# A new order for the first block of a fused FNet mixing and feed-forward kernel

## The chip, the cores and the metric

One core of a Trainium2 chip runs the whole kernel. Time is the device time of one execution in microseconds (us), the median over several executions. Beside it stands a profile of one more execution, taken by the hardware profiler: its span runs from the first to the last instruction.

The engines are TensorE (PE; PEld are its weight loads), VectorE (DVE), ScalarE (ACT), GpSimd (POOL) and SyncE (SP). Each has a queue of its own and works it off in order; semaphores tie them together.

## The reference

For x of 8 batches, 3008 rows and 256 columns, a Fourier transform over rows and columns, of which the real part is kept, and then a feed-forward layer with a squared ReLU:

```
X = np.fft.fft(x, axis=1)
X = np.fft.fft(X, axis=2)
x = X.real.reshape(8 * 3008, 256)
h = np.maximum(x @ w_in, 0.0)        # w_in 256 x 2048
out = h * h @ w_out                  # w_out 2048 x 256
```

## The kernel before

**What is computed in which form.** The transform over the 256 columns is never made by itself: its cosine and sine matrices (`c_all`, `s_n`) are multiplied with `w_in` once, which gives the weights `gh` (three groups of rows: cosine, sine, and a third that is the sine group times −2, called the turn). The transform over the 3008 rows uses symmetries. Rows n and S − n are added and subtracted (the tiles `u`, `v`, `cs`, `od`, `ev`), so that a quarter of the rows is left, and matmuls with tables of cosines and sines give `pz` in PSUM; copies of it are the tiles `zc` and `zs`, one column for each frequency. The first layer is then `gh[0]·zc + gh[1]·zs` for frequency k, and adding `gh[2]·zs` turns the same PSUM tile into the value for frequency S − k.

**Windows.** The frequencies of all batches stand in one row of columns, cut into windows of at most 512 columns (the first has 240). In a window the hidden 2048 rows come in eight steps of two blocks of 128. A step makes `ph` (L834, L835), a relu on ScalarE (L866), the turn matmuls (L857), a second relu, and a square on VectorE (L873). The second layer of a window (L685, tile `po`) is spread between the steps of the next one. Window 0 has its own form: four quads of four blocks each. `quad` (L912, L913) makes cosine and sine parts, `quad_relu` (L925) is one relu of a whole quad, `quad_turn` (L919) the turn, `quad_power` (L929) the square. There are two PSUM tiles for `ph`, so quad 2 waits until the second relu of quad 0 has read its tile.

**The order.** Nothing plans the work: the scheduling is manual and each engine's queue has the order in which the program issues the instructions. The first block is written out by hand:

1. GpSimd issues the load of the first batch's x in four quarters (`load_x`: two by one direct transfer, L127, two by gathers, L132), then `w_in` (L179) and later `w_out` (L318).
2. The tables of cosines and sines. For each angle n·k the whole turns are taken off: `args` (L231, ScalarE) scales and rounds, `turns` (L237) makes −S times the number of turns, `mods` (L243, VectorE) is n·k plus that, in three instructions for each of two halves. `sins` (L249, ScalarE) takes the sine. `weigh` (L270, ScalarE) scales one row of the sines. `coss` gets the cosines from the sines: a matmul with a mask that reverses the partitions (`perm`, L259, tile `pc`) and a copy (L260).
3. `idle` issues matmuls whose result nobody reads (L296, tile `pw`).
4. The fold of the first batch: `u_odd` (L388 to L390: quarter 0 minus 1, quarter 2 minus 3), `u_part` (L393, then L362, which gives `od`), a copy of one column of `od` on ScalarE (L396, the edge), `nyq` (two tiny matmuls and L444).
5. The matmuls `pz` of the first unit (L569). Each of the parts 0 (cosine) and 1 (sine) has two halves; between them ScalarE copies the first to `es` (L574), and behind them to `zc` or `zs` (L580 for window 0, L587 for window 1). `minus` (L598) gives the second half of the unit's columns.
6. The weights: `gh_step` (L515 matmuls `pg`; L505 scales on VectorE, L503 on ScalarE) for four groups of 512 columns, and `gh_turn` (L522).
7. `v_even` (L399) makes `v` and at its end issues the load of the next batch's x, which goes into the same tile. `d_even` (L419, L420) is the first to read that.

In window 1 the squares are kept back in a list: `settle` issues all that are in it. The steps of the next batch's fold lie between them, up to `nyq` (L444), which the matmuls `pz` of the second unit wait for.

Of the kernel before, what the change touches and what calls it, by code (L numbers as in the profile page):

```python
# [16 lines left out]
P = 128  # L17
# [12 lines left out]
def kernel(  # L30
# [130 lines left out]
    def iota(shape, pattern, base, mult, name):  # L161
        t = const.tile(shape, I32, name=name)
        nc.gpsimd.iota(t, pattern=pattern, base=base, channel_multiplier=mult)
        return t
# [9 lines left out]
        idx["r"] = iota([P, 1], [[1, 1]], P - 1, -1, "idx_r")  # L174

    xs = {0: load_x(0, idx_first)}
    w16 = [wp.tile([P, 2, F // 2], F16, name=f"w16_{i}", tag="w16") for i in range(2)]
    for i in range(2):
        nc.gpsimd.dma_start(out=w16[i], in_=moe_w_in[:, i * F // 2 : (i + 1) * F // 2].rearrange("(c p) f -> p c f", p=P))  # L179
# [2 lines left out]
    def small(shape, name):  # L182
        return const.tile(shape, F32, name=name)
# [22 lines left out]
    def table_steps(e):  # L206
# [28 lines left out]
        def turns(h, eng=nc.vector):  # L235
            t = st["t", h]
            eng.tensor_scalar(out=t[:, 0:nr, 0:n], in0=t[:, 0:nr, 0:n], scalar1=-R23, scalar2=-float(S), op0=ALU.add, op1=ALU.mult)  # L237

        def mods(h):
            m = st["m", h] = tmp.tile([P, 3, NE], F32, name="m", tag="tm")  # L240
            for j in range(nr):
                r = row(h, j)
                nc.vector.scalar_tensor_tensor(out=m[:, j, 0:n], in0=st["kf"], scalar=vec[:, r : r + 1], in1=st["t", h][:, j, 0:n], op0=ALU.mult, op1=ALU.add)  # L243
# [18 lines left out]
        def weigh():  # L262
            if e:
                for t in (cos_t, sin_t):
                    for r in range(2):
                        nc.vector.tensor_scalar(out=t[:, r, :], in0=t[:, r, :], scalar1=wge[:, r : r + 1], scalar2=None, op0=ALU.mult)
                return

            q = RQ.index(1)
            nc.scalar.activation(sin_t[:, q, :], sin_t[:, q, :], AF.Copy, bias=0.0, scale=wgt)  # L270

        return {"freq": freq, "args": args, "turns": turns, "mods": mods, "absm": absm, "sins": sins, "coss": coss, "weigh": weigh}

    to = table_steps(0)
    to["freq"]()
# [17 lines left out]
    def idle(n):  # L293

        for i in range(n):
            nc.tensor.matmul(pw[:, 0 : 3 * P], spn[:, 0, 0, :], spn.rearrange("p c r d -> p (c r d)")[:, 0 : 3 * P], start=True, stop=True)  # L296

    idle(34)
    to["args"](0)
    to["args"](1)  # L300
    wd = 2.0 * math.pi / D
    s_n = const.tile([P, 2, P + 1], F16, name="s_n")
    nc.scalar.activation(s_n, am, AF.Sin, bias=0.0, scale=-wd)
    c_all = const.tile([P, 2, P + 1], F16, name="c_all")
    nc.scalar.activation(c_all, at, AF.Sin, bias=halfpi[:, 0:1], scale=-wd)
    nc.scalar.activation(s_n[:, :, 0:1], c_all[:, :, P : P + 1], AF.Copy, bias=0.0, scale=0.5)

    to["turns"](0)
    to["mods"](0)
    to["turns"](1, nc.gpsimd)  # L310
    nc.gpsimd.tensor_scalar(out=wgt, in0=nraw[:, 1:2], scalar1=float(Q), scalar2=-0.5, op0=ALU.is_equal, op1=ALU.mult)
    nc.gpsimd.tensor_scalar(out=wgt, in0=wgt, scalar1=1.0, scalar2=None, op0=ALU.add)

    prow_i = iota([P, P], [[1, P]], 0, 1, "prow_i")
    perm = [const.tile([P, P], F16, name=f"perm{i}") for i in range(2)]
    for i in (1, 0):
        nc.gpsimd.tensor_scalar(out=perm[i], in0=prow_i, scalar1=float(P - 1 - i), scalar2=None, op0=ALU.is_equal)
    nc.gpsimd.dma_start(out=wout16, in_=moe_w_out.rearrange("(c p) o -> p c o", p=P))  # L318
    pick = const.tile([P, 1], F16, name="pick")
    nc.gpsimd.memset(pick, 0.0)  # L320
    nc.gpsimd.memset(pick[0:1, :], -2.0)
    evec_i = iota([P, 2], [[1, 2]], 0, 2, "evec_i")
    idx["c"] = iota([P, 1], [[1, 1]], P - 1, -1, "idx_c")
    nc.gpsimd.memset(idx["c"][0:2, :], P - 3)
# [10 lines left out]
    nc.gpsimd.tensor_tensor(wge, wge, wg2, op=ALU.add)  # L335
    nc.gpsimd.tensor_scalar(out=wg2, in0=evec, scalar1=0.0, scalar2=-0.5, op0=ALU.is_equal, op1=ALU.mult)
    nc.gpsimd.tensor_tensor(wge, wge, wg2, op=ALU.add)
    to["sins"](0)
    to["weigh"]()
    to["mods"](1)  # L340
    to["sins"](1)
    to["coss"](0)
    idle(4)
    to["coss"](1)
    to["coss"](2)
    idle(5)

    folded = {}

    fe = fo = None  # L350
# [13 lines left out]
    def fold_steps(i):  # L364
# [19 lines left out]
            fof = fo.rearrange("p q c d -> p (q c) d")  # L384


        def u_odd():
            nc.vector.tensor_tensor(u[:, 0], t[:, 0], t[:, 1], op=ALU.subtract)  # L388
            nc.vector.tensor_copy(t[0:1, 2, 0, :], t[0:1, 0, R - 1, :])
            nc.vector.tensor_tensor(u[:, 1], t[:, 2], t[:, 3], op=ALU.subtract)  # L390

        def u_part(sg):
            nc.vector.tensor_tensor(cs[:, sg], u[:, 0], rev_dim(u[:, 1], 1), op=ALU.subtract if sg else ALU.add)  # L393
            d_fold(od[:, sg], cs[:, sg], sg)
            if not sg:
                nc.scalar.activation(od[:, 0, :, 0:1], cs[:, 0, :, 0:1], AF.Copy, bias=0.0, scale=1.0)  # L396

        def v_even():
            nc.vector.tensor_tensor(v, tq[:, :, 0], tq[:, :, 1], op=ALU.add)  # L399
# [94 lines left out]
            nc.vector.tensor_copy(spn[:, :, :, 0:1], rev_dim(yt[:, :, 0, :, 128:129], 1))  # L494

        late = [lambda: fold8(0), lambda: fold8(1), lambda: fold16(0), lambda: fold16(1), nyq8]
        return {"u_odd": u_odd, "u_part": u_part, "v_even": v_even, "v_part": v_part, "d_even": d_even, "n_cos": n_cos, "odds": odds, "d_odd": d_odd, "load": load, "n_sin": n_sin, "nyq": nyq, "even": even, "away": away, "back": back, "late": late}

    gh = const.tile([P, 3, F], F16, name="gh")

# [19 lines left out]
    def gh_turn(cc):  # L520
        f0 = cc * 512
        nc.vector.tensor_scalar(out=gh[:, 2, f0 : f0 + 512], in0=gh[:, 1, f0 : f0 + 512], scalar1=turn2[:, 0:1], scalar2=None, op0=ALU.mult)  # L522
# [105 lines left out]
    def run(*jobs):  # L628
        for j in jobs:
            j()  # L630

    f0s = fold_steps(0)
    z0 = z_steps(need[0][0], late=True)
    run(f0s["u_odd"], lambda: f0s["u_part"](0))
    run(*z0(0, 0))
    gh_pg = gh_step(0)
    run(lambda: f0s["u_part"](1), f0s["nyq"])
    gh_scale(gh[:, 0:2, 0:512], gh_pg, False)
    run(*z0(0, 1))
    run(*z0(1, 0))  # L640
    run(*z0(1, 1))
    gh_step(1, False)
    turn2 = small([P, 1], "turn2")
    nc.vector.tensor_scalar(out=turn2, in0=dvec[:, 0:1], scalar1=0.0, scalar2=2.0, op0=ALU.is_equal, op1=ALU.mult)
    nc.vector.tensor_scalar(out=turn2, in0=turn2, scalar1=-2.0, scalar2=None, op0=ALU.add)
    gh_turn(0)
    gh_turn(1)

    def store(osb, p0, g0, m, minus, eng=nc.sync):

# [145 lines left out]
    for w in range(NW):  # L796
# [109 lines left out]

        def quad(p):
            ph = phs[p] = ps_h.tile([P, 2, 512], F32, name="ph", tag="psh")
            for c in range(4):
                f0 = (4 * p + c) * P  # L910
                o = ph[:, c // 2, (c % 2) * wn : (c % 2 + 1) * wn]
                nc.tensor.matmul(o, gh[:, 0, f0 : f0 + P], zcw[:, 0:wn], start=(c % 2 == 0), stop=False, skip_group_check=True)  # L912
                nc.tensor.matmul(o, gh[:, 1, f0 : f0 + P], zsw[:, 0:wn], start=False, stop=True, skip_group_check=True)  # L913

        def quad_turn(p):
            for c in range(4):
                f0 = (4 * p + c) * P
                o = phs[p][:, c // 2, (c % 2) * wn : (c % 2 + 1) * wn]
                nc.tensor.matmul(o, gh[:, 2, f0 : f0 + P], zsw[:, 0:wn], start=False, stop=True, skip_group_check=True)  # L919
# [9 lines left out]
            nc.vector.tensor_tensor(h, h, h, op=ALU.mult)  # L929

        if w == 0:
            rm = z0(0, 2) + z0(1, 2)
            run(lambda: quad(0), lambda: quad_relu(0, 0), lambda: quad(1), lambda: quad_relu(1, 0), f0s["v_even"])
            run(lambda: quad_turn(0), lambda: quad_relu(0, 1), lambda: gh_step(2, True), lambda: gh_turn(2))
            run(lambda: quad_power(0), lambda: quad_turn(1), lambda: quad_relu(1, 1), *rm[0::2])
            run(lambda: quad(2), lambda: quad_relu(2, 0), lambda: gh_step(3, False), lambda: gh_turn(3), lambda: quad_power(1))
            run(lambda: quad(3), lambda: quad_relu(3, 0), *rm[1::2])
            run(lambda: quad_turn(2), lambda: quad_relu(2, 1), lambda: quad_power(2), lambda: quad_turn(3), lambda: quad_relu(3, 1), lambda: quad_power(3))
        elif w == 1:
            zl = [j for zu, part, h in zj for j in zu(part, h)]  # L940
            for p in range(NST // 2):
                s0, s1 = 2 * p, 2 * p + 1
                f2q = spread(f2, p, NST // 2)
                n = len(f2q) // 4
                pq(s0)
                if p < 2:
                    settle()
                relu(s0, 0)
                pq(s1)
                relu(s1, 0)  # L950
                if s1 == NST - 1:
                    run(*post[s0 - 1])
                    settle()
                    power(s1, 0, 1)
                    run(*zl)
                run(*f2q[0:n])
                turn(s0)
                run(*f2q[n : 2 * n])
                turn(s1)
                relu(s0, 1)  # L960
                relu(s1, 1)
                run(*at[s0], *at[s1], *f2q[2 * n :])
                if p == 2:
                    settle()
                keep(s0, 0, 2)
                keep(s1, int(s1 == NST - 1), 2)
            gh_nyq()
# [68 lines left out]
```

## Time and profile before

| | us |
|---|---|
| three runs: median (lowest to highest) | 603.12 (602.83 to 603.47) |
| the profiled execution | 602.28 |
| its span, first to last instruction | 600.5 |
| TensorE busy in it | 585.7 (98%) |
| VectorE, ScalarE, GpSimd busy | 497.4, 458.5, 242.5 |
| first matmul of pz | at 15.48 |
| first relu of window 0, end of its last | 20.93, 31.14 |
| window 1's first matmul | at 30.34 |

The mean granted TensorE clock was 0.997 of full speed. A row of a timeline has the start and length in us, engine, line, operation, what is written from what, the tile's shape and the count; in brackets stands the idle time before it and what ended it. A row of the chain of waits has start, length, engine, tile and line. A row of the waits has who waited for whom, the sum in us, how often, and the longest.

### The profile page before, as it was taken

The numbers are of one execution on the slowest core, as the hardware profiler recorded it, in microseconds if no ns is written. First come the engines' busy times: TensorE is split into PE (matmuls) and PEld (weight loads), VectorE is DVE, ScalarE is ACT, GpSimd is POOL, SyncE is SP. The second block draws the span as 40 slices with busy tenths as digits, with TensorE's granted clock in tenths as the row PEclk, the third lists the DMA queues.
The fourth block names the chain that finished last, engine by engine and source line by source line (L and its number), as shares of the span: only waits on it lengthen the run. The fifth ranks groups of instructions, "written<-read, shape, count | busy, mean of one in ns | idle before, by whom it ended". The sixth has DMA issues, their size and how long they took to land.

```text
span 600.5 us, 11262 instructions
## 1 busy us (share of the span) xinstructions
PE 585.7 (98%) x4415; PEld 424.2 (71%) x4415; DVE 497.4 (83%) x594; ACT 458.5 (76%) x613; POOL 242.5 (40%) x285
## 2 busy tenths in 40 slices
PE   7899999999999999999999999999999999999997
PEld 3457776677776767777777777777777777777786
DVE  8787688997989878969899798988899888889871
ACT  6687777967887877778778778777877787787762
POOL 8311355078415515183153641445505724325210
PEclk8999999999999999999999999999999999999999
DMA  8946421127212461273123711146212321212212
GB/s 149 151 85 151 119 74 44 43 84 171 65 38 59 112 155 45 70 151 104 40 62 100 164 47 52 47 118 143 64 34 86 86 63 36 61 41 54 61 55 70
DMA packets 37624, 50.33 MB, mean 84 GB/s; under 512 B 4589, under 2 KB 30755, under 8 KB 37571
## 3 DMA queue, kind: packets, MB, share of 16 engines
q0 software_dynamic: 10400, 24.94, 20.5%
q1 hardware_dynamic: 26899, 24.44, 13.6%
q8 instruction: 34, 0.56, 0.4%
q10 hardware_dynamic: 272, 0.23, 0.1%
q14 instruction: 19, 0.16, 0.1%
HBM read 36.42 MB, written 27.86 MB: 107 GB/s over the span
## 4 chain that ended last, share of the span: by engine, by line
PE 80%; DVE 11%; ACT 4%; issue 2%; DMA 1%; POOL 1%; ACTq 0%; DVEq 0%; POOLq 0%
PE po L685 47%; PE ph L857 6%; PE ph L834 6%; PE ph L835 6%; PE ph L852 5%; PE ph L843 5%; PE pz L569 4%; DVE h L873 3%; DVE t L847 2%; DVE h L864 2%; ACT h L866 2%; DMA xo<-in_x_dram,idx_r 1%; ACT h L877 1%; DVE zc L598 1%; DVE zs L598 1%
## 5 line engine op out<-in xcount | busy, mean ns | idle before, releaser
L685 PE MATMUL po<-wout,h 128*128 128x256 f16 (+1 forms) x3024 | 363.5, 273 | 0.0
L685 PEld LDWEIGHTS <-h 128*128 128x128 f16 (+1 forms) x3024 | 296.7, 98 | 73.5
L866 ACT ACTIVATE h<-ph 128x1024 f16<-128x1024 f32 (+3 forms) x303 | 288.9, 991 | 60.9 <-PE ph L852 37.3
L873 DVE TENSOR_TENSOR h<-h 128x2048 f16<-128x2048 f16 (+7 forms) x201 | 194.4, 973 | 19.1 <-ACT h L866 15.8
L793 POOL TENSOR_SCALAR n<-zn,g2n 128x512 f32<-128x512 f16 (+3 forms) x162 | 160.4, 1004 | 73.4 <-DMA zn<-rd 53.7
L847 DVE SCALAR_TENSOR_TENSOR t<-ph,n 128x1024 f32<-128x1024 f32 (+3 forms) x81 | 96.4, 1190 | 34.7 <-PE ph L843 31.4
L864 DVE CUSTOM_DVE_ANT_0 h<-t,ph 128x1024 f16<-128x1024 f32 x71 | 86.5, 1218 | 22.8 <-ACT h L866 20.0
L700 ACT ACTIVATE osb<-po 128x512 f32<-128x512 f32 (+3 forms) x95 | 55.0, 582 | 51.7 <-PE po L685 43.9
L785 POOL DMA_DIRECT2D zn<-rd x22 | 12.8, 584 | 179.1 <-DMA rd<-zs 179.1
L834 PE MATMUL ph<-zc,gh 128*128 128x512 f16 (+3 forms) x222 | 81.9, 369 | 2.1 <-DVE zc L598 1.1
L877 ACT ACTIVATE h<-h 128x1024 f16<-128x1024 f16 (+3 forms) x81 | 83.8, 1034 | 0.3
L835 PE MATMUL ph<-zs,gh 128*128 128x512 f16 (+3 forms) x222 | 81.9, 369 | 0.0
L857 PE MATMUL ph<-zs,gh 128*128 128x512 f16 (+3 forms) x222 | 63.8, 369 | 0.0
L852 PE MATMUL ph<-zs,gh 128*128 128x512 f16 (+3 forms) x162 | 47.0, 372 | 1.5 <-issue 0.5
L843 PE MATMUL ph<-zc,gh 128*128 128x512 f16 (+3 forms) x162 | 47.1, 372 | 0.0
L834 PEld LDWEIGHTS <-gh 128*128 128x128 f16 x222 | 21.6, 97 | 25.1 <-DVE zc L598 1.4
L835 PEld LDWEIGHTS <-gh 128*128 128x128 f16 x222 | 21.7, 98 | 24.2 <-issue 1.5
L843 PEld LDWEIGHTS <-gh 128*128 128x128 f16 x162 | 15.8, 98 | 18.4 <-issue 0.7
L857 PEld LDWEIGHTS <-gh 128*128 128x128 f16 x222 | 20.6, 98 | 3.5
L453 POOL DMA_DIRECT2D scr<-ev x8 | 4.7, 590 | 40.8 <-DVE ev L449 34.9
L463 POOL DMA_INDIRECT rb<-scr,idx_r x16 | 18.3, 1141 | 4.9 <-issue 4.9
L574 ACT ACTIVATE es<-pz 128x376 f32<-128x376 f32 (+1 forms) x32 | 14.8, 485 | 7.0 <-PE pz L569 6.8
(141 smaller groups left out, 366.0 us busy)
## 6 DMA issues: line engine op xcount, KB each, us to landing
out_dram<-osb SPq DMA_DIRECT2D x77, 128.0 KB
xo<-in_x_dram POOLq DMA_DIRECT2D x7, 768.0 KB
scr<-ev POOLq DMA_DIRECT2D x8, 390.0 KB
zn<-rd POOLq DMA_DIRECT2D x19, 128.0 KB
rb<-scr POOLq DMA_DIRECT2D x16, 130.0 KB
out_dram<-osb SPq DMA_DIRECT2D x12, 94.0 KB
w<-in_moe_w_in_dram POOLq DMA_DIRECT2D x2, 512.0 KB
wout<-in_moe_w_out_dram POOLq DMA_DIRECT2D x1, 1024.0 KB
```

What stands on the lines that cost most here:

```text
L685: nc.tensor.matmul(po[0:m, j * D : (j + 1) * D], h2[:, fc, q : q + m], wout16[:, fc, :], start=(fc == 0 and not both), stop=(fc == NFC - 1 ...
L793: nc.gpsimd.tensor_scalar(out=n2[:, a, 0:wn1], in0=zns[wt][:, 0:wn1], scalar1=g2n[:, fc : fc + 1], scalar2=1.0, op0=ALU.mult, op1=ALU.mult)
L834: nc.tensor.matmul(ph[:, a, 0:wn], gh[:, 0, f0 : f0 + P], zcw[:, 0:wn], start=True, stop=False)
L835: nc.tensor.matmul(ph[:, a, 0:wn], gh[:, 1, f0 : f0 + P], zsw[:, 0:wn], start=False, stop=True)
L843: nc.tensor.matmul(ph[:, a, 0:wn], gh[:, 0, f0 : f0 + P], zcw[:, 0:wn], start=True, stop=True)
L847: nc.vector.scalar_tensor_tensor(out=t2[:, :, 0:wn], in0=phs[s][:, :, 0:wn], scalar=-2.0, in1=n2s[w, s][:, :, 0:wn], op0=ALU.mult, op1=ALU ...
L852: nc.tensor.matmul(phs[s][:, a, 0:wn], gh[:, 1, f0 : f0 + P], zsw[:, 0:wn], start=False, stop=True, skip_group_check=True)
L857: nc.tensor.matmul(phs[s][:, a, 0:wn], gh[:, 2, f0 : f0 + P], zsw[:, 0:wn], start=False, stop=True, skip_group_check=True)
L864: nc.vector._custom_dve(TENSOR_ADD_SAT, out=h, in0=t2s[s][:, :, 0:wn], in1=phs[s][:, :, 0:wn], s0=BIG, s1=0.0)
L866: nc.scalar.activation(h, phs[s][:, :, 0:wn], AF.Relu, bias=0.0, scale=-1.0)
L873: nc.vector.tensor_tensor(h, h, h, op=ALU.mult)
L877: nc.scalar.activation(h, h, AF.Square, bias=0.0, scale=1.0)
```

## The change

- **Angles.** For the second half of the angles the instructions of `mods` go. `kns` makes n·k on ScalarE (three copies with a scale), `sums` adds the turns on GpSimd in one instruction over the whole tile.
- **Other engines.** `weigh` goes from ScalarE to GpSimd; the two instructions for `wgt` and the two masks `perm` go from GpSimd to VectorE; `turn2` (two tiny instructions) from VectorE to GpSimd. The iota `prow_i` is issued ahead of the load of `w_in`; `w_out` is issued behind `weigh`.
- **Fold.** `u_odd` is cut into `u_half` (quarters 0 and 1, and the copy of one row) and `u_odd` (quarters 2 and 3). `coss` is issued behind `u_part(0)`; the edge copy becomes a step of its own, behind `coss`.
- **TensorE.** 44 idle matmuls instead of 34 ahead of the first `coss`.
- **Weights and unit.** `gh_turn(0)` and `gh_step(1)` are issued between the two halves of part 1 of `pz`; the copies of `zc` and `zs` for window 1 directly behind the half whose result they read, ahead of window 0; `v_even` behind `gh_turn(1)`, ahead of window 0.
- **Window 0.** A quad makes its four cosine matmuls first and then its four sine matmuls. `gh_step(2)` goes ahead of the first turn, `gh_step(3)` ahead of quad 2, and both are scaled on VectorE. The four squares come at the end.
- **Window 1.** Behind the third pair of steps one kept square is issued instead of all that are kept (two at that point).

```diff
     xs = {0: load_x(0, idx_first)}
+    prow_i = iota([P, P], [[1, P]], 0, 1, "prow_i")
...
+        def kns(h):
+            m = st["m", h] = tmp.tile([P, 3, NE], F32, name="m", tag="tm")
+            for j in range(nr):
+                r = row(h, j)
+                nc.scalar.activation(m[:, j, 0:n], st["kf"], AF.Copy, bias=0.0, scale=vec[:, r : r + 1])
+
+        def sums(h):
+            m = st["m", h][:, 0:nr, 0:n]
+            nc.gpsimd.tensor_tensor(m, m, st["t", h][:, 0:nr, 0:n], op=ALU.add)
...
             q = RQ.index(1)
-            nc.scalar.activation(sin_t[:, q, :], sin_t[:, q, :], AF.Copy, bias=0.0, scale=wgt)
+            nc.gpsimd.tensor_scalar(out=sin_t[:, q, :], in0=sin_t[:, q, :], scalar1=wgt[:, 0:1], scalar2=1.0, op0=ALU.mult, op1=ALU.mult)
...
-    idle(34)
+    idle(44)
     to["args"](0)
     to["args"](1)
+    to["kns"](1)
...
-    nc.scalar.activation(s_n[:, :, 0:1], c_all[:, :, P : P + 1], AF.Copy, bias=0.0, scale=0.5)
     to["turns"](0)
     to["mods"](0)
     to["turns"](1, nc.gpsimd)
-    nc.gpsimd.tensor_scalar(out=wgt, ...
-    prow_i = iota([P, P], [[1, P]], 0, 1, "prow_i")
+    to["sums"](1)
+    nc.vector.tensor_scalar(out=wgt, ...
     for i in (1, 0):
-        nc.gpsimd.tensor_scalar(out=perm[i], in0=prow_i, ...
+        nc.vector.tensor_scalar(out=perm[i], in0=prow_i, ...
+    to["sins"](0)
+    nc.scalar.activation(s_n[:, :, 0:1], c_all[:, :, P : P + 1], AF.Copy, bias=0.0, scale=0.5)
+    to["weigh"]()
     nc.gpsimd.dma_start(out=wout16, in_=moe_w_out.rearrange("(c p) o -> p c o", p=P))
...
+    nc.gpsimd.tensor_scalar(out=turn2, ...
...
-    to["sins"](0)
-    to["weigh"]()
-    to["mods"](1)
     to["sins"](1)
-    to["coss"](0)
-    idle(4)
-    to["coss"](1)
-    to["coss"](2)
-    idle(5)
...
-        def u_odd():
+        def u_half():
             nc.vector.tensor_tensor(u[:, 0], t[:, 0], t[:, 1], op=ALU.subtract)
             nc.vector.tensor_copy(t[0:1, 2, 0, :], t[0:1, 0, R - 1, :])
+
+        def u_odd():
             nc.vector.tensor_tensor(u[:, 1], t[:, 2], t[:, 3], op=ALU.subtract)
...
-    run(f0s["u_odd"], lambda: f0s["u_part"](0))
+    run(f0s["u_half"], f0s["u_odd"], lambda: f0s["u_part"](0))
+    to["coss"](0)
+    idle(4)
+    to["coss"](1)
+    to["coss"](2)
+    idle(5)
+    f0s["edge"]()
     run(*z0(0, 0))
     gh_pg = gh_step(0)
     run(lambda: f0s["u_part"](1), f0s["nyq"])
     gh_scale(gh[:, 0:2, 0:512], gh_pg, False)
     run(*z0(0, 1))
     run(*z0(1, 0))
+    gh_turn(0)
+    gh_step(1, False)
+    rm = z0(0, 2) + z0(1, 2)
+    rm[0]()
     run(*z0(1, 1))
-    gh_step(1, False)
-    turn2 = small([P, 1], "turn2")
...
-    gh_turn(0)
+    rm[2]()
     gh_turn(1)
+    f0s["v_even"]()
...
-            for c in range(4):
-                f0 = (4 * p + c) * P
-                o = ph[:, c // 2, (c % 2) * wn : (c % 2 + 1) * wn]
-                nc.tensor.matmul(o, gh[:, 0, f0 : f0 + P], zcw[:, 0:wn], start=(c % 2 == 0), stop=False, skip_group_check=True)
-                nc.tensor.matmul(o, gh[:, 1, f0 : f0 + P], zsw[:, 0:wn], start=False, stop=True, skip_group_check=True)
+            for k, zw in ((0, zcw), (1, zsw)):
+                for c in range(4):
+                    f0 = (4 * p + c) * P
+                    o = ph[:, c // 2, (c % 2) * wn : (c % 2 + 1) * wn]
+                    nc.tensor.matmul(o, gh[:, k, f0 : f0 + P], zw[:, 0:wn], start=(k == 0 and c % 2 == 0), stop=(k == 1), skip_group_check=True)
...
         if w == 0:
-            rm = z0(0, 2) + z0(1, 2)
-            run(lambda: quad(0), lambda: quad_relu(0, 0), lambda: quad(1), lambda: quad_relu(1, 0), f0s["v_even"])
-            run(lambda: quad_turn(0), lambda: quad_relu(0, 1), lambda: gh_step(2, True), lambda: gh_turn(2))
-            run(lambda: quad_power(0), lambda: quad_turn(1), lambda: quad_relu(1, 1), *rm[0::2])
-            run(lambda: quad(2), lambda: quad_relu(2, 0), lambda: gh_step(3, False), lambda: gh_turn(3), lambda: quad_power(1))
-            run(lambda: quad(3), lambda: quad_relu(3, 0), *rm[1::2])
-            run(lambda: quad_turn(2), lambda: quad_relu(2, 1), lambda: quad_power(2), lambda: quad_turn(3), lambda: quad_relu(3, 1), lambda: quad_power(3))
+            run(lambda: quad(0), lambda: quad_relu(0, 0), lambda: quad(1), lambda: quad_relu(1, 0))
+            run(lambda: gh_step(2, False), lambda: gh_turn(2))
+            run(lambda: quad_turn(0), lambda: quad_relu(0, 1), lambda: quad_turn(1), lambda: quad_relu(1, 1))
+            run(lambda: gh_step(3, False), lambda: gh_turn(3))
+            run(lambda: quad(2), lambda: quad_relu(2, 0), lambda: quad(3), lambda: quad_relu(3, 0), *rm[1::2])
+            run(lambda: quad_turn(2), lambda: quad_relu(2, 1), lambda: quad_turn(3), lambda: quad_relu(3, 1), *(lambda p=p: quad_power(p) for p in range(4)))
...
                 if p == 2:
-                    settle()
+                    kept.pop(0)()
```

## The prediction

> **What bounds the kernel now.** I read the page's sums first, then a table of stretches of the span, then the chain of waits through the first 50 us.
>
> ```profile
> span 600.5 us, 11262 instructions
> PE 585.7 (98%) x4415; PEld 424.2 (71%) x4415; DVE 497.4 (83%) x594; ACT 458.5 (76%) x613; POOL 242.5 (40%) x285
> ```
>
> TensorE is busy for nearly all of the span. The columns of the next view are the stretch, then busy time of PE, PEld, DVE, ACT, POOL, the granted clock and the DMA.
>
> ```profile
> 9.95:15.48 5.53, 4.26 (x15) 2.05 (x16) 5.43 (x9) 5.04 (x7) 5.12 (x14) 0.69 1.04 177
> 19.90:30.34 10.44, 8.02 (x58) 5.21 (x57) 8.59 (x16) 7.75 (x12) 2.91 (x3) 1.00 0.84 129
> 50.95:73.20 22.25, 22.25 (x187) 17.61 (x184) 15.92 (x26) 15.50 (x24) 5.11 (x10) 1.00 0.39 115
> ```
>
> From 50.95 us on TensorE has no hole at all, so whatever the change brings or costs has to come from the start and is then carried to the end by an unbroken TensorE queue. Window 0 (19.90 to 30.34) leaves it 2.4 us idle, and before 15.48 it does mostly idle matmuls. The chain says what is waited for there (start, length, what):
>
> ```profile
> 7.31 2.60 DVE m L243 x3
> 9.92 1.15 ACT sin L249
> 11.12 0.76 PE pc L259 x2
> 11.88 1.28 PE pw L296 x4
> 13.16 0.64 PE pc L259 x2
> 13.82 1.49 ACT cos L260 x2
> 15.48 0.65 PE pz L569 x3
> 21.87 1.68 DVE v L399
> 26.39 8.13 DMA xo<-in_x_dram,idx_r
> 45.76 0.67 PE pz L569 x3
> ```
>
> Two points in it carry the rest: the first useful matmul pz at 15.48 (call it t0), which needs the cosines and the folded x, and the pz of the second unit at 45.76, which needs x of the next batch. The change moves t0, and it moves everything between t0 and window 1.
>
> **Part one: up to t0. The angles leave VectorE, but not its port.** Three multiply-adds of L243 go. In their place stand three Copy activations on ScalarE (kns) and one add of two 128x1128 f32 tiles on GpSimd (sums); weigh goes from ScalarE to GpSimd. These rows show what GpSimd does to VectorE:
>
> ```profile
> 7.31 1.54 DVE L243 SCALAR_TENSOR_TENSOR m<-kf,nvec,t 128x376 f32<-128x376 f32 x1
> 7.32 1.13 POOL L237 TENSOR_SCALAR t<-t 128x1128 f32<-128x1128 f32 x1
> 9.81 0.63 DVE L243 SCALAR_TENSOR_TENSOR m<-kf,nvec,t 128x376 f32<-128x376 f32 x1
> ```
>
> The same instruction takes 0.63 us later and 1.54 while GpSimd's pass runs: it ends 0.4 us behind that pass (8.85 against 8.45). VectorE stood still for the whole GpSimd instruction. Much later the other direction:
>
> ```profile
> 76.46 1.34 POOL L793 TENSOR_SCALAR n<-zn,g2n 128x376 f32<-128x376 f16 x1
> 76.51 0.92 DVE L873 TENSOR_TENSOR h<-h 128x1504 f16<-128x1504 f16 x1
> 77.36 0.98 DVE L477 TENSOR_TENSOR xy<-rb 128x1040 f16<-128x1040 f16 x1
> 78.27 0.69 DVE L477 TENSOR_TENSOR xy<-rb 128x1040 f16<-128x1040 f16 x1
> ```
>
> GpSimd waits until the square ends (77.43), runs 0.37 us to 77.80, and the next VectorE instruction is 0.29 longer than its twin. So a waiting GpSimd pass gets in between two VectorE instructions with two tile inputs, and both kinds exclude each other. I therefore add GpSimd's time to VectorE's.
>
> How long the add takes no row shows. The nearest is L237 on GpSimd: the same 1128 elements with one input, 1.13 us. That is the lower bound; twice it, 2.26, is the upper one if the two inputs are read one after the other. I take 2.26, since the port is what both rows above show to be scarce. Nothing excludes a time below the lower bound if the add let VectorE through; that is rival B.
>
> The Trainium skill, "GPSIMD Engine Reference", section "Elementwise — side-by-side cycle accounting", gives 4497 ns for a tensor_tensor add of 2048 f32, because both inputs share one read port; scaled to 1128 elements that is an estimate of 2.48 us, and the forecast below would be 0.2 us higher by it. No row here can confirm it.
>
> ```profile
> 4.02 3.10 ACT L231 ACTIVATE t<-kf,nvs 128x376 f32<-128x376 f32 x6 [1.79 <-DVE kf L223]
> 4.39 0.48 DVE L285 TENSOR_SCALAR at<-irow,dvs 128x129 f32<-128x129 f32 x2
> 11.45 0.94 DVE L388 TENSOR_TENSOR u<-xo 128x1536 f16<-128x1536 f16 x1
> 14.55 0.57 DVE L362 TENSOR_TENSOR od<-cs 128x768 f16<-128x768 f16 x1
> 15.20 0.23 ACT L396 ACTIVATE od<-cs 128x6 f16<-128x6 f16 x1
> ```
>
> VectorE's path: od is done at 15.12 (14.55 + 0.57). Three L243 go, from 9.81 to 11.45: −1.64. Two masks perm (128x128, priced as the two of L285) +0.48 and two tiny instructions for wgt, at most as much, taken as +0.3. The add +2.26, weigh +0.37 (the 128x376 pass at 77.43). od at 16.9; the edge copy on ScalarE and the handover as before, 0.36: t0 = 17.3.
>
> ScalarE's path: kns is 3 of 6 args, 1.55 us, so it ends near 8.7, just as GpSimd is done with its first pass. The add is then waiting when the second L243 ends, and the third comes behind it: the first sine starts at 9.92 + 2.26 = 12.2. From there to t0 took 5.56; weigh leaves ScalarE but the s_n copy takes its place, and TensorE's steps pc, idle, pc set the middle: t0 between 17.3, if the idle matmuls keep the clock up, and 17.7. I take t0 = 17.5, later by 2.0. If the third L243 slips ahead of the add, the sine is early, but u stands behind the add and VectorE's path is unchanged.
>
> So the half of u that is put ahead of x's last quarters starts near 13, where x's later half was already taken without a wait before (L390 ran back to back behind this L388): that piece brings nothing here. The 10 further idle matmuls lie in TensorE's pause and cost nothing; without that pause they would be up to 3.2 us (0.32 each by the chain's x4 at half clock). The iota ahead of w_in, the later wout and turn2 on GpSimd:
>
> ```profile
> GB/s 0 18 115 213 211 213 213 205 135 161 212 193 200 199 159 11 29 80 211 215 211 215 88 5 0 0 0 168 27 137 213 212 217 203 139 77 54 212 96 89
> 10.79 1.23 POOL L318 DMA_DIRECT2D wout<-in_moe_w_out_dram  x1
> 17.04 0.20 POOL L337 TENSOR_TENSOR wge<-wge,wg 128x2 f32<-128x2 f32 x1
> ```
>
> Slices are 1.5 us: the queue is full until 22.5, so w_in stays behind x. wout is issued near 14.2, still with a backlog of w_in ahead of it, and is first used some 30 us in. GpSimd's small instructions, of which L337 is the last, end some 4 us later than before, near 21.5; x of the next batch is issued near 24.2. Cover in each case over 2 us; cost nothing. Behind the add's wait for kns GpSimd queues weigh, wout and turn2. Only weigh is soon wanted: done near 14.2, it is read by the second pc, which comes some 3 us after the first sine starts (13.16 against 9.92 before), at 15.4.
>
> **Part two: from t0 to window 1.**
>
> ```profile
> 18.57 0.64 PE L569 MATMUL pz<-sin,od 128*128 128x376 f16 x3 [0.57 <-ACT es L574]
> 20.93 2.85 ACT L925 ACTIVATE h<-ph 128x960 f16<-128x960 f32 x3 [1.31 <-PE ph L913]
> 23.67 1.09 ACT L503 ACTIVATE gh<-pg 128x512 f16<-128x512 f32 x2
> 28.45 2.69 ACT L925 ACTIVATE h<-ph 128x960 f16<-128x960 f32 x3 [1.61 <-PE ph L913]
> 19.68 1.29 DVE L505 TENSOR_SCALAR gh<-pg 128x512 f16<-128x512 f32 x2 [1.32 <-PE pg L515]
> 21.25 0.62 DVE L522 TENSOR_SCALAR gh<-gh,turn 128x512 f16<-128x512 f16 x2
> 25.07 1.15 DVE L929 TENSOR_TENSOR h<-h 128x1920 f16<-128x1920 f16 x1
> ACT h L925 <- PE ph L913: 2.9, 2, 1.6
> ```
>
> Window 0 is eight relus on ScalarE, about 0.87 us apart where nothing comes between (28.45 + 2.69 for three). Before they fill 20.93 to 31.14: 10.2 us for 7.1 of work. In between lie the two weight copies (1.09), the copies of zc and zs, and the wait of 1.61 for group 2.
>
> First, weight group 1 is now made while the es copy runs, which fills the hole of 0.57; and the cosine half of a quad no longer waits for zs. The first relu comes at t0 + 4.95 instead of t0 + 5.45 (20.93 − 15.48): −0.5.
>
> Then the weights of groups 2 and 3 are scaled on VectorE and stand ahead of the turns, and the zc and zs copies fall into gaps ahead of the relus. VectorE counted on from t0: group 0 until 2.9, turn 0.3, group 1 until 4.4, turn, v 1.7 until 6.4, group 2 (1.29) until 7.6, turn, group 3 until 9.2, turn 9.5. TensorE has quad 2 by 8.9 and quad 3 by 9.8. Relus: 4.95, 5.8, 7.05 (the turn stands behind weight group 2), 7.9, 9.15, 10.0, 10.9, 11.75, the last done at 12.7. Eight take 7.8 instead of 10.2: −2.4. The sum of this part is −2.9 against t0.
>
> Queued behind: the four squares now all follow the last scale and the two minus steps. At 1.1 us each (L929) they are done at 11.6, 12.7, 13.8 and 14.9; the second-layer matmuls that read them come from 13.7 on, one per 0.9 us or slower. Slack 1.6 us at the least; cost nothing, and every us of VectorE beyond that is lost one for one.
>
> **Part three: x of the next batch.** v starts at t0 + 4.65 instead of t0 + 6.4: with t0 at 17.5 the load is issued 0.3 later than before and lands near 34.9 (26.39 + 8.13 = 34.52 before).
>
> ```profile
> 43.26 2.35 DVE L873 TENSOR_TENSOR h<-h 128x2048 f16<-128x2048 f16 x2
> 45.53 0.17 DVE L444 CAST od<-py 128x6 f16<-128x6 f32 x1
> ```
>
> One square instead of two stands ahead of the L444 that pz at 45.76 waits for: −1.17. Together −0.9, the same as TensorE brings along (2.0 − 2.9). The square kept back joins three more behind L444: 4.1 us from 45 on, done near 49, ahead of window 2 at 50.
>
> **Sum.** +2.0 − 2.9 = −0.9 us by the rows. I give back 0.1 for handovers at the new seams: −0.8. The profiled execution took 602.28 us (span 600.5 and what lies around it), 0.84 under the median 603.12 of the three runs. Its time becomes 601.5; on the median's scale 602.3.
>
> **Rivals.** What a measurement of this kernel can tell from no change is about 0.2%, 1.2 us.
>
> A, the forecast: port held for two reads, 602.3.
>
> B, faster: the add costs one read's time, 1.13, or does not stop VectorE at all. For it: the only two-input GpSimd rows are tiny. With 1.13 t0 is 16.4 and the net −1.9: 601.2. With nothing, the older limits hold, t0 near 14.8 (both paths less what was taken away), net −3.5: 599.6. Against it: the 1.54 us row.
>
> C, slower: window 0 gains nothing but the 0.5, because VectorE brings weight groups 2 and 3 too late, with v (1.68) ahead of them and all scales on it. Its price: the 2.4 are gone, +2.0 − 0.5 + 0.1 = +1.6, 604.7. It decides once VectorE reaches group 2 later than t0 + 8.8 (6.4 by my count), since the relus then wait as long as before. For it: VectorE already waited 1.32 at L505; against it: by my count it waits for nothing from t0 + 1.7 to the last square.
>
> D: TensorE's clock. The 2.7 us pause before 11.12 gave a clock of 0.69 over 9.95 to 15.48; that is half speed for 3.4 of the 5.53 us. A pause of over 3 us may put that stretch onto pz and weight group 0: up to +1.7, 604.0.
>
> **Chances.** A 0.47, B 0.32, C 0.12, D 0.09. Faster by over 0.2% comes from B and the lower edge of A: 0.40. Slower: most of C, half of D and a little of A's upper edge: 0.18. The rest, 0.42, is within 0.2%. A's own range is 601.3 to 603.4. The whole range reaches to 600.0, between B's two cases, and to 604.3, past D and short of C.
>
> **What would show it.** Right: the add on GpSimd over 2 us long, with one L243 or the first u stretched by as much; the first pz between 17 and 18; eight relus in 8 us; L444 near 45. Wrong: a first pz before 16.5 (B), relus still over 9.5 us from first to last (C), or half clock behind the first pz (D). A new hole of TensorE behind window 2 would break the premise that only the start counts.

## The result, and the profile after

The changed kernel takes 602.00 us (median of 18 runs, 600.60 to 602.48), the kernel before 603.01 in the same series: the ratio is 0.9981, 95% interval 0.9974 to 0.9989, a gain of 1.0 us. The forecast was 0.8 us. The profiled execution has a span of 600.0 us against 600.5:

```profile
span 600.0 us, 11286 instructions
```

The chain of waits of the changed kernel (start, length, what), lines renumbered by the change: L254 is the multiply-add (L243 before), L260 the sine, L270 pc, L580 pz, L943 the relu of a quad, L455 the cast (L444 before).

```profile
7.44 4.90 DVE m L254 x3
12.44 1.15 ACT sin L260
13.63 0.48 PE pc L270 x2
...
17.89 0.48 PE pz L580 x3
...
27.01 2.70 ACT h L943 x3
```

Three multiply-adds took 2.60 us before and take 4.90 now, and the first sine starts at 12.44 instead of 9.92. The timelines of VectorE and GpSimd say why:

```profile
7.44 1.54 DVE L254 SCALAR_TENSOR_TENSOR m<-kf,nvec,t 128x376 f32<-128x376 f32 x1
8.91 2.91 DVE L254 SCALAR_TENSOR_TENSOR m<-kf,nvec,t 128x376 f32<-128x376 f32 x1
...
7.46 1.13 POOL L238 TENSOR_SCALAR t<-t 128x1128 f32<-128x1128 f32 x1
8.79 2.62 POOL L248 TENSOR_TENSOR m<-m,t 128x1128 f32<-128x1128 f32 x1 [0.21 <-ACT m L244]
```

The new add (L248) is in flight from 8.79 to 11.41. The second multiply-add, nominally from 8.91, ends at 11.82, 0.41 us behind it, a little less than the 0.55 that such an instruction takes by itself (three in 1.64 us before the change, from 9.81 to 11.45). It stood still for nearly the whole add. The next rows, from the timelines of TensorE, VectorE and ScalarE, follow the delay through window 0 and window 1:

```profile
17.73 0.64 PE L580 MATMUL pz<-cos,od 128*128 128x376 f16 x3
...
22.56 1.75 DVE L410 TENSOR_TENSOR v<-xo 128x3072 f16<-128x3072 f16 x1
24.23 1.28 DVE L516 TENSOR_SCALAR gh<-pg 128x512 f16<-128x512 f32 x2
28.31 4.36 DVE L947 TENSOR_TENSOR h<-h 128x1920 f16<-128x1920 f16 x4
44.79 0.18 DVE L455 CAST od<-py 128x6 f16<-128x6 f32 x1
...
22.64 1.83 ACT L943 ACTIVATE h<-ph 128x960 f16<-128x960 f32 x2 [0.48 <-PE ph L931]
27.01 3.56 ACT L943 ACTIVATE h<-ph 128x960 f16<-128x960 f32 x4 [0.45 <-PE ph L931]
...
45.04 0.65 PE L580 MATMUL pz<-sin,od 128*128 128x376 f16 x3 [0.29 <-DVE od L455]
```

| | before | after | against its own first pz, before and after |
|---|---|---|---|
| first pz | 15.48 | 17.73 | |
| first relu of window 0 | 20.93 | 22.64 | 5.45, 4.91 |
| end of the last relu | 31.14 | 30.57 | 15.66, 12.84 |
| window 1's first matmul | 30.34 | 29.76 | 14.86, 12.03 |
| pz of the second unit | 45.76 | 45.04 | 30.28, 27.31 |

The first block loses 2.25 us up to the first pz and wins 2.8 to 3.0 back behind it.

### The profile page after: what moved, and what is told of

It is laid out like the page before. It is cut to its first block, busy times and chain, and to the rows that moved or that the text cites. A ratio compares the mean times of both kernels' runs of the same rounds, so it can differ in the third digit from the quotient of the medians.

```text
span 600.0 us, 11286 instructions
## 1 busy us (share of the span) xinstructions
PE 586.3 (98%) x4425; PEld 425.5 (71%) x4425; DVE 499.1 (83%) x595; ACT 457.9 (76%) x613; POOL 243.3 (41%) x285
## 4 chain that ended last, share of the span: by engine, by line
PE 82%; DVE 11%; ACT 4%; issue 2%; POOL 0%; DMA 0%; ACTq 0%; DVEq 0%; POOLq 0%
PE po L703 46%; PE ph L852 7%; PE ph L875 7%; PE ph L853 7%; PE ph L870 5%; PE ph L861 5%; PE pz L580 4%; DVE h L891 3%; DVE t L865 2%; ACT h L884 2%; DVE h L882 2%; DVE m L254 1%; ACT h L895 1%; DVE zc L609 1%; DVE zs L609 1%
```

## The experiments

Theory P is the prediction's: a GpSimd pass shuts VectorE out for its length, so part one costs about 2 us, and part two gains about 2.9. Its rival N: the port is not the cause and work on GpSimd is free. All ratios are to the kernel before, which ran on the same chip beside each; the changed kernel's 0.9981 is the mark to compare with. 0.1% is 0.6 us.

### e1: the same add on VectorE

```diff
-            nc.gpsimd.tensor_tensor(m, m, st["t", h][:, 0:nr, 0:n], op=ALU.add)
+            nc.vector.tensor_tensor(m, m, st["t", h][:, 0:nr, 0:n], op=ALU.add)
```

> The changed kernel with the one add (sums) on VectorE instead of GpSimd; all else stays. Theory P (GpSimd's add shuts VectorE out for its whole length, as the profile after shows with one multiply-add of 2.91 us beside an add of 2.62): the add costs VectorE about 1.3 us (1128 f32 elements, two inputs) instead of standing still for 2.6. The first sine starts near 10.0 instead of 12.44, since all three multiply-adds go ahead of the add, and the first pz near 15.7 to 16.0 instead of 17.73. The time is 1.5 to 2.0 us under the changed kernel, so 2.5 to 3.0 under before (ratio 0.995 to 0.996). Theory N (VectorE was slow in that place for another reason, and GpSimd's work was free): VectorE has 1.3 us more to do and the time is 1.3 us above the changed kernel, 0.3 above before (ratio 1.0005).

600.26 us, ratio 0.9951 (0.9937 to 0.9966). Timelines of VectorE and TensorE:

```profile
7.64 2.39 DVE L254 SCALAR_TENSOR_TENSOR m<-kf,nvec,t 128x376 f32<-128x376 f32 x3
9.96 1.32 DVE L248 TENSOR_TENSOR m<-m,t 128x1128 f32<-128x1128 f32 x1
...
15.70 0.64 PE L580 MATMUL pz<-cos,od 128*128 128x376 f16 x3 [0.88 <-DVE od L370]
```

The add costs VectorE 1.32 us when it makes it itself and 2.4 when GpSimd does. One word moved from engine to engine is worth 0.3%, 1.8 us, although the busier engine does the work now. N is out.

Not all of the 1.8 us is GpSimd's hold on VectorE. The first half of u starts 1.06 us earlier (11.71 instead of 12.77), but the first pz 2.03 (15.70 instead of 17.73): the sines come earlier, TensorE's pause ahead of the first pc shrinks from 3.78 to 0.55 us, and its clock stays up, which alone is worth 0.8 at the first pz (e6 has the same angles as the changed kernel and full clock, and its first pz at 16.95). Compared with those runs of the changed kernel that had the full clock (table under e9), e1 is 1.05 us shorter.

### e2: the add twice on GpSimd

```diff
             nc.gpsimd.tensor_tensor(m, m, st["t", h][:, 0:nr, 0:n], op=ALU.add)
+            twin = fop.tile([P, 3, NE], F32, name="twin", tag="rb")[:, 0:nr, 0:n]
+            nc.gpsimd.tensor_tensor(twin, m, st["t", h][:, 0:nr, 0:n], op=ALU.add)
```

> The changed kernel with a second add of the same size on GpSimd directly behind the first, into a tile that nobody reads. Theory P: the second one shuts VectorE out again for 2.6 us, now in front of the first half of u; the first pz comes 2 to 2.6 us later than 17.73, and as TensorE has no hole from window 2 on, all of it reaches the end: 2 to 2.6 us over the changed kernel, 1 to 1.6 over before (ratio 1.0017 to 1.0027). Theory N: no change against the changed kernel (ratio 0.998 to before). A third reading, that the start is covered by the load of the next batch's x: the first pz is later but the time is not.

605.46 us, ratio 1.0040 (1.0025 to 1.0055). Timelines of VectorE and GpSimd (L256 is the multiply-add, L250 the second add):

```profile
7.44 7.21 DVE L256 SCALAR_TENSOR_TENSOR m<-kf,nvec,t 128x376 f32<-128x376 f32 x3
...
8.79 2.63 POOL L248 TENSOR_TENSOR m<-m,t 128x1128 f32<-128x1128 f32 x1 [0.19 <-ACT m L244]
11.50 2.75 POOL L250 TENSOR_TENSOR twin<-m,t 128x1128 f32<-128x1128 f32 x1
```

The three multiply-adds now last 7.21 us. It had been expected that the second add would run behind all three, ahead of u; it did not wait so long. The second multiply-add (8.92 to 11.83) ended between the two adds, and the third one (11.75 to 14.65) ended 0.40 us behind the second add. The first pz moved from 17.73 to 20.34 (+2.61) and the second unit's pz from 45.04 to 47.76 (+2.72): a delay in the first block is not absorbed. The time rose by 0.59%, 3.5 us, more than the 2.6 expected. The profiled spans differ by 3.4: 2.7 are there by the second unit's pz, 2.9 by the last copy out of PSUM (599.05 against 596.13), and 0.5 lies behind that copy, where the last result is stored. That last part is not explained.

### e3 and e4: each part alone

e3 keeps the angles, masks and weigh of the change and takes the order of before from the first pz on; e4 the reverse, with 34 idle matmuls. Window 0, its quads and the place of `turn2` go with their side. Their cores, e3 against the changed kernel and e4 against the kernel before:

```diff
# e3
-    gh_turn(0)
-    gh_step(1, False)
-    rm = z0(0, 2) + z0(1, 2)
-    rm[0]()
     run(*z0(1, 1))
-    rm[2]()
+    gh_step(1, False)
+    gh_turn(0)
     gh_turn(1)
-    f0s["v_even"]()
...
-                    kept.pop(0)()
+                    settle()
# e4
+    gh_turn(0)
+    gh_step(1, False)
+    rm = z0(0, 2) + z0(1, 2)
+    rm[0]()
     run(*z0(1, 1))
+    rm[2]()
     gh_turn(1)
+    f0s["v_even"]()
...
-                    settle()
+                    kept.pop(0)()
```

> Part one of the change alone: kns and sums, weigh on GpSimd, wgt and perm on VectorE, 44 idle matmuls, the fold's steps; from the first pz on, the order of before. By the prediction's sum part one costs about 2.0 us (first pz at 17.7 instead of 15.48): 2.0 to 2.3 over before, ratio 1.0033 to 1.0038. Theory N: no difference to before or a small gain (ratio 0.998 to 1.000).

> Part two of the change alone: angles, masks, weigh and 34 idle matmuls as before; from the first pz on the new order (weights ahead of the turns, v ahead of window 0, one kept square). By the prediction's sum this part gains 2.9 us: first pz at 15.48, first relu near 20.4, the last relu's end near 28.3 instead of 31.14, time 2.5 to 3.0 under before, ratio 0.995 to 0.996. If the gain of window 0 needed the new angles (rival), it is under 1.5 us: ratio 0.9975 or more.

e3: 605.02 us, ratio 1.0027 (1.0016 to 1.0037). e4: 600.68 us, ratio 0.9957 (0.9940 to 0.9973). Part one alone costs 1.6 us by the ratio, part two alone gains 2.6. Together they would make −1.0; the whole change made −1.1. The parts add up within the intervals, and the first one alone makes the kernel slower. e3 cost less than the 2.0 to 2.3 us expected (its interval, 1.0 to 2.2, reaches them); e4 is in the range expected.

e4's profile also brought the prediction's rival D, the clock, which P alone does not explain. Timeline of TensorE, then rows of the table by stretch (third number from the end: the granted clock):

```profile
15.72 1.14 PE L572 MATMUL pz<-cos,od 128*128 128x376 f16 x3
16.66 1.06 PE L518 MATMUL pg<-w,c_all 128*128 128x512 f16 x2
...
12.00:13.00 1.00, 0.55 (x4) 0.22 (x3) 0.97 (x3) 1.00 (x2) 0.86 (x5) 0.66 1.12 186
13.00:14.00 1.00, 0.79 (x3) 0.25 (x2) 0.96 (x2) 1.00 (x2) 0.94 (x5) 0.50 0.98 121
...
18.00:19.00 1.00, 1.00 (x6) 0.44 (x5) 0.36 (x2) 0.00 (x0) 0.00 (x0) 0.50 1.44 197
19.00:20.00 1.00, 1.00 (x7) 0.59 (x6) 0.94 (x1) 0.44 (x2) 0.00 (x0) 0.93 1.47 201
```

TensorE ran at half speed from 12.3 to 19.1 us, over the first pz and weight group 0; the first relu came 6.6 us behind the first pz instead of 4.9. The gain of part two was partly hidden in this execution, and in two more: three of e4's six runs have a mean clock of 0.994, the other three of 0.999 or 1.0, and the median span of the first three is 1.7 us longer (599.8 against 598.1).

### e5: e4 with 44 idle matmuls

```diff
-    idle(34)
+    idle(44)
```

> The kernel of e4 (part two alone, angles as before) with 44 idle matmuls instead of 34. In e4's profile TensorE ran at half clock from 12.4 to 19.1 us, over the first pz and weight group 0: pg came every 0.53 us instead of 0.22, and the first relu started 6.6 us behind the first pz instead of 4.9. Clock theory (rival D of the prediction): with the longer row of idle matmuls TensorE's pause ahead of the first pc is near 1 us instead of 2.1, the clock stays up, pg is at 0.22 and the first relu 4.9 us behind the first pz. Time 0.5 to 1.5 us under e4's median (600.7), runs closer together than e4's 2.0 us. Rival: e4's slow stretch has nothing to do with the pause; no difference to e4.

599.86 us, ratio 0.9948 (0.9934 to 0.9961), five runs within 0.5 us (e4's six within 2.0).

```profile
15.26 0.64 PE L572 MATMUL pz<-cos,od 128*128 128x376 f16 x3 [0.43 <-DVE od L365]
15.73 0.59 PE L518 MATMUL pg<-w,c_all 128*128 128x512 f16 x2
```

Full clock, first relu at 20.17, 4.9 behind the first pz. TensorE's pause was 1.23 us instead of 2.12. So in this place ten more matmuls that nobody reads are worth 0.8 us by the medians (0.5 by the ratios), and part two with the clock kept up gains 3.1 us. What they do is keep the clock up in every run: all five have a mean clock of 0.998 or more, and their median span is 598.1, the same as that of e4's three runs at full clock.

### e6: both kept squares issued again

```diff
                 if p == 2:
-                    kept.pop(0)()
+                    settle()
```

> The changed kernel with both kept squares issued behind the third pair of steps of window 1, as before the change. The prediction counts 1.17 us for this at the L444 cast that the second unit's pz waits for (L455 in the changed kernel, at 44.9): it moves to 46.0, pz from 45.04 to 46.1 to 46.2, and the time rises by 1.0 to 1.1 us (ratio to before 0.9995 to 1.0003). Rival: pz's hole is filled from elsewhere or given back in window 2, and the time stays within 0.3 us of the changed kernel (ratio 0.998 to 0.9985).

602.65 us, ratio 1.0000 (0.9991 to 1.0010): 1.1 us given back by the ratio, 0.65 by the medians. The medians mix runs of different clocks; of runs with the same clock e6 is 1.1 to 1.3 us longer than the changed kernel (table under e9). The pz of the second unit shows where:

```profile
45.60 0.33 PE L580 MATMUL pz<-sin,od 128*128 128x376 f16 x1 [1.62 <-DVE od L455]
```

It waits 1.62 us for the cast instead of 0.29. Without this one line about 1.1 us of the gain in window 0 would have been spent waiting for the next batch's fold.

### e7: window 0 alone in its old order

```diff
+            run(lambda: quad_turn(0), lambda: quad_relu(0, 1), lambda: gh_step(2, True), lambda: gh_turn(2))
+            run(lambda: quad_power(0), lambda: quad_turn(1), lambda: quad_relu(1, 1))
+            run(lambda: quad(2), lambda: quad_relu(2, 0), lambda: gh_step(3, False), lambda: gh_turn(3), lambda: quad_power(1))
...
-            run(lambda: gh_step(2, False), lambda: gh_turn(2))
-            run(lambda: quad_turn(0), lambda: quad_relu(0, 1), lambda: quad_turn(1), lambda: quad_relu(1, 1))
-            run(lambda: gh_step(3, False), lambda: gh_turn(3))
```

> The changed kernel with window 0 alone in the order of before: weight group 2 behind the first turn and scaled on ScalarE, group 3 behind quad 2, squares between; v, the copies of zc and zs and weight group 1 stay where the change puts them. The prediction counts 2.4 us for the new order of window 0, of which the two copies (0.3) stay gained here: eight relus fill 9.9 to 10.2 us instead of 7.9, window 1 starts 2.0 to 2.3 later, time 1.5 to 2.3 us above the changed kernel (ratio to before 1.001 to 1.002). The load of the next x is as early as in the changed kernel, so the cast ahead of the second unit's pz is not late; if that load and not TensorE's arrival decides (rival), the time rises by under 0.8 us.

604.09 us, ratio 1.0020 (1.0010 to 1.0030): 2.1 us over the changed kernel by the medians. Timeline of ScalarE:

```profile
23.03 2.70 ACT L943 ACTIVATE h<-ph 128x960 f16<-128x960 f32 x3 [0.48 <-PE ph L931]
25.60 1.10 ACT L514 ACTIVATE gh<-pg 128x512 f16<-128x512 f32 x2
26.55 1.88 ACT L943 ACTIVATE h<-ph 128x960 f16<-128x960 f32 x2
30.25 2.69 ACT L943 ACTIVATE h<-ph 128x960 f16<-128x960 f32 x3 [1.82 <-PE ph L931]
```

The eight relus fill 9.9 us again (23.03 to 32.94) against 7.9 in the changed kernel; the two weight copies and the wait for group 2 are back in between.

### e8 and e10: all angles on VectorE, then weigh back on ScalarE

```diff
# e8, on top of e1
-    to["turns"](1, nc.gpsimd)
+    to["turns"](1)
-    nc.vector.tensor_scalar(out=wgt, ...       (both, and the two of perm)
+    nc.gpsimd.tensor_scalar(out=wgt, ...
# e10, on top of e8
-            nc.gpsimd.tensor_scalar(out=sin_t[:, q, :], in0=sin_t[:, q, :], scalar1=wgt[:, 0:1], ...
+            nc.scalar.activation(sin_t[:, q, :], sin_t[:, q, :], AF.Copy, bias=0.0, scale=wgt)
```

> The kernel of e1 with GpSimd's other pass over the angles (turns of the second half, 1.13 us, which held up one multiply-add for 0.97 us) on VectorE as well, and wgt and perm back on GpSimd. Theory P: VectorE loses the stand-still of 1.0 and the 0.75 of wgt and perm, gains a pass of 0.6 to 1.1 with one input, and is stopped a few tenths by perm on GpSimd; the first half of u starts 0.3 to 0.8 us earlier than e1's 11.71, the first pz 0.2 to 0.7 earlier than 15.70. Time 599.6 to 600.1. Theory N (work on VectorE costs, work on GpSimd does not): 0.3 to 0.8 us above e1's 600.3.

> The kernel of e8 with weigh on ScalarE as before the change. In e8 weigh waits on GpSimd from 10.55 to 12.36 and stretches the one-row copy in the fold from 0.21 to 0.53 us, and VectorE's od is what the first pz (15.17) waits for, while ScalarE's cosines are done 0.8 earlier. Theory P: od 0.3 earlier, first pz near 14.85, time 0.2 to 0.4 under e8 (599.2 to 599.4). Rival: weigh's 0.6 us on ScalarE delays sines and cosines more than VectorE gains; no gain or a loss of up to 0.3.

e8: 599.57 us, ratio 0.9944 (0.9931 to 0.9958). e10: 599.38 us, ratio 0.9936 (0.9921 to 0.9952); runs of either within 0.6 us. First pz of e8 and of e10, and weigh in e8 on GpSimd:

```profile
15.17 0.64 PE L580 MATMUL pz<-cos,od 128*128 128x376 f16 x3 [0.84 <-DVE od L370]
...
10.55 1.81 POOL L281 TENSOR_SCALAR sin<-sin,wgt 128x376 f16<-128x376 f16 x1 [0.61 <-ACT s_n L330]
11.91 0.53 DVE L397 COPY xo<-xo 1x256 f16<-1x256 f16 x1
```

```profile
14.85 0.64 PE L580 MATMUL pz<-cos,od 128*128 128x376 f16 x3 [0.52 <-DVE od L370]
11.91 0.21 DVE L397 COPY xo<-xo 1x256 f16<-1x256 f16 x1
```

With no pass over the angles on GpSimd the first pz comes at 15.17, and at 14.85 once weigh is off GpSimd too, the copy shrinking from 0.53 to 0.21 us as expected. Both kernels beat the kernel before and the changed one: e10 the kernel before by 3.4 us (medians 599.38 and 602.75) and the changed one, by the ratios, by 0.45%. The step from e8 to e10 (0.2 us) is of the size expected, but can't be told from none by the intervals.

### e9: TensorE's pause in the changed kernel filled

```diff
-    idle(44)
+    idle(64)
```

> The changed kernel with 64 idle matmuls instead of 44: the 20 more, 0.16 us each at full clock, end near 13.2, just ahead of the first pc at 13.63, so TensorE's pause of 3.8 us shrinks to about 0.5. Clock theory: no half speed from the first pc on; the first pz comes near 17.0 instead of 17.73 (as in e6, whose profile shows full clock and 16.95); the median falls by 0.3 to 0.8 us against the changed kernel (ratio to before 0.9968 to 0.9977) and the runs lie within 0.7 us of each other instead of 1.9. Rival: the spread comes from elsewhere (transfers, say): no smaller spread and no gain.

601.74 us, ratio 0.9979 (0.9969 to 0.9989), twelve runs from 600.91 to 602.86. The profile does what the clock theory says: the pause is 0.22 us, the clock full throughout, the first pz at 16.60.

```profile
13.30 0.48 PE L270 MATMUL pc<-sin,perm 128*128 128x376 f16 x2 [0.22 <-ACT sin L260]
...
16.60 0.65 PE L580 MATMUL pz<-cos,od 128*128 128x376 f16 x3 [0.20 <-ACT od L407]
```

By device time the expectation missed: the spread is 1.95 us, no smaller than before, and the gain of 0.3 us by the medians can't be told from none by the ratios. The other numbers of the runs say why. Of every run the span and the mean clock granted to TensorE over it are on record. 3.4 us at half speed, as in the changed kernel's profile, cost 1.7 of 600 us and so make a mean of 0.997. The runs divide by it:

| | TensorE's pause ahead of the first pc, by the profile | runs at 0.998 or more, median span | runs at 0.997 or less, median span |
|---|---|---|---|
| e9 | 0.22 | 12, 599.6 | none |
| e1 | 0.55 | 5, 598.5 | none |
| e5 | 1.23 | 5, 598.1 | none |
| e4 | 2.12 | 3, 598.1 | 3, 599.8 |
| e6 | 3.00 | 6, 600.65 | 5, 601.8 |
| the changed kernel | 3.78 | 6, 599.55 | 12, 600.5 |

The kernel before ran beside each with medians of 602.75 to 603.19 us, so differences of a few tenths between rows mean little. But in the changed kernel no run of one group reaches into the other (598.8 to 599.9 and 600.0 to 600.7), so about half of the spread of its runs, 1.9 us, is the clock, and half speed costs it about 0.9 us. With the pause filled all twelve runs are in the first group and as long as that group was. The gain is there in the spans, 0.6 us by the medians (599.6 against 600.2). It does not arrive in the device time: that is 1.7 to 1.8 us more than the span in every run of the other kernels, but up to 3.3 in e9, in six of its twelve runs more than elsewhere. Why is open.

## Why the prediction was right

**What bounds it.** That only the start counts held: window 2 begins 0.72 us earlier (50.23 against 50.95) and the span is 0.5 shorter. That TensorE has no hole from 50.95 us on was read from a row that ends at 73.20; behind it TensorE is idle for 3.4 us in the kernel before, longest in this wait, which the changed kernel has too (1.05 us, at 91.94):

```profile
92.73 0.39 PE L834 MATMUL ph<-zc,gh 128*128 128x512 f16 x1 [1.05 <-DVE zc L598]
```

So the queue is not unbroken, and of the 0.72 us only 0.46 are left at the last copy out of PSUM (596.13 against 596.59). That a shift at the start reaches the end holds nearly, as e2 shows: +2.6 at the first pz, +2.7 at the second unit's, +2.9 at the last copy.

**Part one, +2.0.** First pz at 17.73 against the forecast 17.5 (+2.25), and the part alone +1.6 to +1.8 us of time (e3). The term of the add was taken at 2.26 us from twice a one-input pass. From the end of the first multiply-add (8.98) to the add's end (11.41) are 2.43, so it was 0.17 too small. The estimate of 2.48 from the Trainium skill, "GPSIMD Engine Reference", section "Elementwise — side-by-side cycle accounting", was nearer; this trace agrees with it. Other terms were too large: wgt and the masks took VectorE 0.51 us instead of 0.78, and weigh held it up by some 0.26 (the second half of u takes 1.22 instead of 0.96) instead of 0.37. So od was done at 16.70 where 16.9 was counted. One detail was off: the add got in after the first multiply-add, not after the second. The prediction's own figures say so, with kns done near 8.7 and the first multiply-add at 8.85. The sum is the same, as the two exclude each other in either order. The piece called worthless stayed so: the first half of u starts at 12.77, back to back with the work before it.

**The clock, within part one.** The forecast gave 17.3 for a clock kept up and 17.7 without. The changed kernel's profile has half clock ahead of the first pz and 17.73; the profile of e6, with the same part one and full clock, has 16.95 (e9's has 16.60, but there u already starts 0.33 us earlier, at 12.44). The direction was right and the size, 0.4, too small: 0.8 us. Rival D, half clock over pz and weight group 0, is what e4's profile shows; in the changed kernel's it ends near 17.6, ahead of the first pz.

**Part two, −2.9.** −2.6 in e4, −3.1 in e5 with the clock kept up. First relu at first pz + 4.91 (forecast 4.95), eight relus in 7.93 us (7.8). VectorE waits for nothing from 19.30 to 32.7, and the squares end at 32.67, 14.9 behind the first pz, as counted: rival C's place, VectorE late with groups 2 and 3, did not come about.

**Part three.** The cast at 44.79 and its pz at 45.04, 0.72 earlier than before (forecast 0.9). e6 confirms the square at 1.1 to 1.3 us: without that line the time is that of before, by the ratio.

**The sum.** −0.8 forecast, −1.0 measured. It came out near because both big terms were near, not because little happened: +1.6 to +2.25 and −2.6 to −3.1 nearly cancel. But there is luck in how near. Against 603.01 of the kernel before, the twelve runs with half speed gained 0.75 us (median 602.26) and the six without 1.7 (601.34), twice the forecast. The forecast took t0 between the two clocks. With the clock up the first pz came 0.35 us earlier than counted (16.95 against 17.3), and half speed then cost twice what was counted: two errors of opposite sign, and the median lies between the groups.

## What to carry to other kernels

Before work is moved to GpSimd to relieve VectorE, look in the trace for a VectorE instruction with two inputs that is longer beside a GpSimd pass than elsewhere: if it is longer by the pass, GpSimd's time belongs in VectorE's sum, and a two-input pass can cost more there than on VectorE itself, as this add does (2.4 us against 1.32). A change of several parts that nearly cancel should be taken apart: here one part alone was a gain of 0.4 to 0.5%, and the other hid more than half of it. Before two medians are compared, sort the runs by granted clock: here that explained about half of a spread of 1.9 us, and part of what e1 and e5 gained. A gain in one stage is kept only if what the next stage waits for comes as early, as the one kept square shows.

## What the runs showed of the hardware that was not expected

**GpSimd does not always get in at the next seam.** In e8 weigh stood ready from 10.55 us; the VectorE add ended at 11.12, but the next VectorE instruction, u, went ahead, and weigh, which needs some 0.4 us (an estimate from the 0.37 of the pass of the same shape that the prediction shows), ended at 12.36, next to the copy that came after; which of the two went first the records do not tell. In the changed kernel the waiting add got in at once, after the first multiply-add.

**Half speed comes in pieces of 3.4 us.** In the changed kernel it fills parts of four 1 us stretches:

```profile
14.00:15.00 1.00, 1.00 (x5) 0.44 (x4) 1.00 (x1) 1.00 (x2) 1.00 (x2) 0.57 1.09 203
...
17.00:18.00 1.00, 1.00 (x6) 0.51 (x5) 0.97 (x2) 0.49 (x2) 0.85 (x5) 0.72 1.17 122
```

With the two rows of 0.50 between them that is (0.43 + 0.5 + 0.5 + 0.28) / 0.5 = 3.4 us; in e4 it is about 6.8, twice as much. It is not fixed by the program: of the changed kernel's 18 runs six show none, and e6, with the same first part and a pause of 3.0 us, shows none in its profile. The pause does bear on it: in the kernels whose profiles have a pause of 1.23 us or less (e1, e5, e8, e9, e10) none of 32 runs has a mean clock under 0.998, with 2.12 us (e4) three of six have. The Trainium skill, "TensorE: Matmul & The Clock Gate", section "Part 1: The HAM clock gate", says that activity is judged in free-running windows of 3413 ns that do not start with the kernel; these lengths agree with it.
